# Sliding-window attention and a squared-ReLU MLP on one core: one quarter-megabyte of attention output turned by DMA, in a new order of work

## The chip, the core and the metric

The kernel runs on one core of a Trainium2 chip. A core has TensorE (PE, matrix products and transposes through a 128x128 array), VectorE (DVE), ScalarE (ACT), GpSimd (POOL) and SyncE (SP, which only issues transfers here), and 16 DMA engines. Each engine has its own instruction queue and works through it in order. The metric is the device time of one execution in microseconds (us), lower is better; several runs are made and the median is given.

## The reference

Four batches, eight heads, 768 tokens, head size 64. Each token attends to the 128 latest tokens and to the first four (the sinks). The heads' outputs are put side by side, 512 numbers a token, and go through two matrix products with a squared ReLU between them.

```python
scores = scale * np.matmul(q, k.transpose(0, 1, 3, 2))
keep = is_sink | in_window            # first 4 tokens, or 0 <= i - j < 128
a = softmax(np.where(keep, scores, -1e9))
x = np.matmul(a, v)                   # [4, 8, 768, 64] -> [3072, 512]
h = x @ w_in                          # 512 -> 2048
g = np.maximum(h, 0.0) ** 2
out = g @ w_out                       # 2048 -> 512, float32
```

## The kernel before

**Tiles.** A batch has six tiles of 128 tokens, taken in three pairs, s = 0, 1, 2; tokens 512 to 767 are s = 2. Everything is computed in bf16 and summed in f32.

**Attention of a batch.** Q and K come as [tokens, heads x 64] and must be turned, because a product needs the head dimension on the partitions. For batches 0 and 1 TensorE turns them (`pt`, L642; input `qs` for the first four tiles of batch 0, loaded by SP and cast by DVE, else `qn`, loaded and cast by POOL's queue), and DVE or ACT copies the result to `qkT`. For batches 2 and 3 (`NATURAL`) SP issues a DMA transpose (L596). Then TensorE makes the scores (`ps`, L749; for the first pair of batch 0 with a bias, L742), ACT their exponential (`expm`, L769), DVE or POOL the mask (L778, L781 on DVE; two instructions of L360 on POOL), and TensorE the products with V (`po`, L817), which carry the sum of weights as a 65th column. The sinks have scores of their own (`pk`, L708), exponentials (`es`), and V rows (`vs`, L690). DVE divides by the sum and writes the attention output to `xn_sb` (L833, L834).

**The bridge.** The first product of the MLP needs the attention output with its 512 features on the partitions. For batches 0 and 1 TensorE turns each pair of tiles with eight 128x128 transposes (`px`, L866), and two copies by DVE or ACT bring them to `xT`. For batches 2 and 3 SP issues two DMA transposes for a pair (L848).

**The MLP.** Layer 1 (`pm`, L895) runs in blocks of 128x1024 numbers in PSUM: with two pairs of tokens at once (512 wide, 8 matmuls of 512 columns) or with one (256 wide, 16 matmuls of 256 columns). A block goes through a ReLU (`r`, L906 on ACT, L908 on DVE) and a square (`gT`, L915 on ACT, L917 on DVE). Layer 2 is plain for the first two pairs of batch 0 (`py`, L936) and otherwise a Strassen-like scheme with seven products instead of eight (`py`, L1047; for the very last pair one of them in a bank of its own, `ya`), whose sums and differences (`sg`, `wt`, L1005, L977) and combinations (`u`, `osb`, L1072, L1088, L1095) DVE makes. SP stores each pair of tiles as 512 KB (L959, L1120); the last pair of the last batch is stored in parts (L1113, L1114, L1125, L1129).

**What sets the order.** Every step is an operation in a list, with a key, the engines that may do it and a cost on each, the steps that it comes after and the buffers that it takes. A planner (`Plan.run`) walks through them at build time and always takes the operation that can start first by its own clock, ties by key; where several engines may do a step it takes the one that ends it first. The result is a fixed order for every queue. The planner's clock adds `LATENCY` when a result goes from one engine to another, and gives each DMA a time on its queue, `DMA_LATENCY` and a `margin` of its own:

```python
start = max([t + slack if t > 0 else 0.0, engine.get(e, 0.0)] +
            [a.end + LATENCY + slack for a in o.after if a.engine != e or a.dma] +
            [a.issued for a in o.follow])
...
cand = (round(pick[1] + o.lag, 2), o.key)
...
queue[e] = max([queue.get(e, 0.0), end + DMA_START[e]] + moved) + o.dma
end = queue[e] + DMA_LATENCY + o.margin
```

`PLACES` shifts and stretches the keys of a group of steps and gives it a `lag`; `NUDGES` does so for single operations, by their number in the list. While the planner's clock is below `WARM_UNTIL`, it fills gaps on TensorE with transposes whose results nobody reads (L327).

**The loads.** POOL's queue carries, in this order: V of batch 0 and the four slices of `w_in` (512 KB each) mixed, K and Q of batch 0's tiles 4 and 5 (`load_cast`, 128 KB a tile), the rest of batch 0's V, four parts of `w_out` (512 KB each), K and Q of batch 1's tiles 0 to 3, its V for them, K and Q of its tiles 4 and 5, its last V, then batches 2 and 3. Issues wait once eight of them are under way. `load_cast` gives each of its loads 0.9 us on the queue, and a margin of 1.2 for batch 0, 0.3 for batch 1.

Of the kernel before, what the change touches and what calls it, by code (L numbers as in the profile page):

```python
# [16 lines left out]
LATENCY = 0.135  # L17
# [5 lines left out]
    ('att', 0, 0): (3.3, 1.08, 0.18), ('att', 0, 1): (3.285, 0.47, 0.38), ('att', 0, 2): (-0.2, 1.41, -0.24),  # L23
    ('att', 1, 0): (-1.415, 2.2, -0.42), ('att', 1, 1): (-0.385, 1.02, -0.22), ('att', 1, 2): (6.08, 1.06, 0.36),
    ('att', 2, 0): (-0.225, 0.25, -0.64), ('att', 2, 1): (-1.615, 1.17, -0.58), ('att', 2, 2): (0, 1.02, -0.06),
    ('att', 3, 0): (-0.075, 1.08, 0.1), ('att', 3, 1): (-0.04, 1.04, 0.04), ('att', 3, 2): (1.235, 0.72, 0.98),
    ('ev', 0, 2): (-0.16, 1.15, 0.78), ('ev', 1, 0): (0.585, 0.56, -0.48), ('ev', 1, 1): (0.47, 1.11, 0.24),
    ('ev', 1, 2): (-0.095, 1.18, 0.08), ('ev', 2, 0): (-0.22, 0.93, 0.28), ('ev', 2, 1): (0.015, 1.02, -0.46),
    ('ev', 2, 2): (1.345, 0.4, 1.32), ('ev', 3, 1): (-0.155, 1, 0.08), ('ev', 3, 2): (-0.055, 1.28, -0.44),
    ('l1', 0, 0): (-0.035, 1.27, 0), ('l1', 0, 1): (0.18, 0.85, 0.08), ('l1', 0, 2): (-0.6, 1.31, -0.4),  # L30
    ('l1', 1, 0): (4.96, 0.3, 0.74), ('l1', 1, 2): (0.265, 1.41, -0.28), ('l1', 2, 0): (-0, 0.59, 0.5),
    ('l1', 2, 2): (0.1, 1.22, -0.12), ('l1', 3, 0): (0.075, 0.91, 0.48), ('l2', 0, 0): (0.055, 0.81, 0.38),
    ('l2', 0, 1): (0.435, 1.16, 0), ('l2', 0, 2): (0.16, 1.12, -0.1), ('l2', 1, 0): (1.05, 0.56, -0.96),
    ('l2', 1, 1): (-0.425, 1.06, -0.1), ('l2', 1, 2): (-0.18, 1.03, 0.2), ('l2', 2, 0): (-0.115, 0.96, 0.58),
    ('l2', 2, 1): (2.185, 1.21, 1.32), ('l2', 2, 2): (2.75, 1, 0.74), ('l2', 3, 0): (-0.765, 0.25, 2.4),
    ('l2', 3, 1): (0.08, 0.81, 0.18), ('l2', 3, 2): (0.23, 1.94, 2.82), ('prep', 0, 0): (2.165, 1.2, -0.5),
    ('prep', 0, 1): (0.115, 1.01, -0.24), ('prep', 1, 0): (0.05, 0.87, 0.08), ('prep', 1, 1): (0.84, 1.23, 0.54),
    ('prep', 2, 0): (-0.005, 0.96, 0.24), ('prep', 3, 0): (-0.045, 1.08, 1.16),
    ('sink', 0, 0): (0.015, 1.11, -0.04), ('sink', 0, 1): (0, 1.12, -0.06), ('sink', 1, 0): (-0.225, 1.01, -0.06),
    ('sink', 3, 0): (-0.565, 0.62, 0.5), ('sum', 0, 2): (-0.14, 0.68, -0.34), ('sum', 1, 0): (-1.615, 0.44, -1.74),  # L40
    ('sum', 1, 1): (0.645, 0.91, -1.4), ('sum', 1, 2): (0.34, 1.45, 0.14), ('sum', 2, 0): (-0.655, 1.85, 0.06),
    ('sum', 2, 1): (-0.24, 1, 0.18), ('sum', 2, 2): (0.405, 1.27, 0.3), ('sum', 3, 0): (0.25, 2.36, 0.94),
    ('sum', 3, 2): (0.185, 1.17, 1.74), ('turn', 0, 0): (-0.56, 2.1, -0.62), ('turn', 0, 1): (0.11, 0.94, -0.14),
    ('turn', 0, 2): (-0.205, 1.01, 0.02), ('turn', 1, 0): (-0.2, 0.94, -0.02),
    ('turn', 1, 1): (-0.345, 1.33, -0.42), ('turn', 1, 2): (1.765, 2.5, -2.14), ('turn', 2, 0): (0, 1.05, 0),
    ('turn', 2, 1): (-0.26, 1.09, -0.3), ('turn', 3, 0): (-0.06, 1.05, -0.44), ('turn', 3, 1): (0.075, 0.56, 0.64),
    ('turn', 3, 2): (0, 1, 0.14), ('val', 0, 0): (0.345, 0.45, -0.28), ('val', 0, 1): (0.69, 0.58, -0.46),
    ('val', 0, 2): (-0.09, 0.78, -0.08), ('val', 1, 0): (-2.595, 0.7, 0.22), ('val', 1, 1): (0.035, 1.14, 0.06),
    ('val', 1, 2): (-0.65, 0.98, 0.64), ('val', 2, 0): (-1.11, 0.59, -1.94), ('val', 2, 1): (0.755, 0.42, -0.3),
    ('val', 2, 2): (-0.425, 1.6, -0.06), ('val', 3, 0): (0.1, 1.17, 0.6), ('val', 3, 1): (0.805, 0.25, 0.74),  # L50
    ('val', 3, 2): (0.105, 0.92, 2.28), ('wt', 0): (-0.205, 0.82, -0.32),
}
NUDGES = {
    4: (-0.022, 0.56), 16: (0, 0.14), 17: (-0.211, -0.38), 18: (0.48, -1.62), 19: (0, 0.4), 20: (0.364, -0.58),
    21: (0.004, 0.16), 22: (0.02, 0), 23: (0.016, 0.18), 24: (-0.06, -0.78), 25: (0.35, 1.84), 26: (-0.106, 0.66),
    27: (0.014, -0.64), 29: (-0.004, 0.86), 30: (0, 0.42), 31: (0.013, 0), 33: (-0.009, 0), 34: (-0.094, 0.5),
    36: (-0.027, 0.16), 37: (0.188, 0.08), 38: (-0.052, 0), 39: (-0.269, -0.82), 40: (-0.004, 0),
    41: (-0.419, 0.34), 42: (0.398, -2.86), 43: (0.134, -0.1), 44: (0.027, 0.14), 45: (0.009, 0), 46: (0.123, 0.66),
    47: (0.073, 0.9), 49: (0, 0.1), 51: (-0.102, -0), 52: (-0.278, -0.06), 53: (-0.001, 0.18), 56: (0.05, 0.1),
    57: (0.049, -0.16), 58: (0.016, -0.78), 60: (-0.008, -0.14), 61: (-0.013, 0), 62: (0, 0.22), 63: (-0.292, -0.2),  # L60
    64: (-0.079, 0.34), 65: (0.028, 0.64), 66: (-0.114, -0.38), 67: (0.099, -0.02), 68: (0.076, -0.28),
    69: (-0.851, 0.68), 71: (0.036, 0.22), 72: (-0.036, -0.24), 73: (0.024, 0.18), 74: (0.02, 0), 75: (-0.063, 0),
    76: (0, -0.04), 78: (0.042, 0.28), 80: (0.009, 0.26), 81: (0.023, 1.36), 82: (-0.02, 0.04), 83: (-0.008, -0.54),
    84: (-0.128, -0.42), 85: (-0.161, -0.36), 86: (0.003, 0), 87: (-0.004, 0.08), 88: (-0.069, 0),
    89: (-0.003, -0.16), 90: (-0.088, 0.02), 91: (0.016, -0.28), 92: (0.109, 0), 93: (0.015, 0.38),
    94: (0.043, -0.24), 95: (0.159, 0.04), 96: (-0.083, 0.04), 97: (-0.05, -0.3), 98: (-0.346, 0.8),
    99: (-0.435, 0.54), 100: (-0.21, -0.52), 101: (0.407, 1.44), 102: (0.013, 0.78), 103: (0.147, -0.08),
    104: (-0.112, -0.16), 105: (-0.121, -0.1), 107: (0.009, 0), 108: (0.214, 0.04), 109: (0.006, 0.08),
    111: (0.033, 0.86), 112: (0.046, 0.56), 113: (0.043, 0.6), 114: (-0.154, 0.42), 115: (-0.084, -0.16),
    116: (-0.145, -0.28), 117: (-0.026, -1.22), 118: (0.126, -0.62), 119: (-0.123, -0.24), 120: (0.115, 0.56),  # L70
    121: (0, -0.14), 122: (-0.121, 0.08), 123: (0, -0.2), 124: (0.034, -0.16), 125: (-0.168, 0.24),
    126: (0.017, -0.44), 127: (0.071, -0.82), 128: (-0.128, 0.1), 129: (-0.006, -0.08), 130: (0, -0.56),
    131: (0.402, 0.04), 132: (-0.056, 0), 133: (0.291, -0.28), 134: (-0.028, 0), 135: (0.064, -1.52),
    136: (-0.069, 0), 137: (-0.061, 0.54), 139: (-0.041, 0.32), 140: (-0.043, 0), 142: (-0.077, -0.12),
    143: (-0.069, 0.14), 144: (0.271, 0.26), 145: (0.008, 0.02), 146: (0.046, -0.52), 147: (0.008, -0.22),
    148: (0.006, 0.26), 149: (-0.028, 0.28), 150: (0.065, 0.06), 151: (0.051, 0.04), 152: (0.164, -0.12),
    153: (-0.401, 0.06), 154: (0.019, 0), 155: (-0.388, -0.64), 156: (-0.112, 1.16), 157: (0.287, 0.94),
    158: (-0.278, 1.3), 159: (-0.002, -0.18), 160: (0.118, 0.3), 162: (0.145, 0.5), 164: (0.158, 0.46),
    165: (0.095, 0), 166: (0.015, 0.02), 167: (0.055, 0), 168: (0.161, -0.48), 169: (-0.217, 0.24),
    171: (0.132, 0.52), 172: (0.011, -0.1), 173: (-0.036, 0.78), 174: (-0.047, -0.16), 175: (0.115, 0),  # L80
    176: (-0.342, 0.18), 177: (0, -0.02), 178: (-0.092, 0.58), 179: (0.041, 0.04), 180: (0.136, 0),
    186: (0.353, 0.28), 187: (-0.073, -0.02), 188: (-0.044, 0.48), 189: (-0.009, 0.06), 190: (0.057, -0.6),
    191: (-0.512, 1.18), 192: (0.405, 0.62), 193: (-0.012, -0.02), 194: (-0.003, 0.04), 195: (0.216, 0.94),
    196: (-0.08, -0.04), 197: (-0.038, 0.14), 198: (0.002, -0.54), 199: (0.12, 0.14), 200: (-0.304, 0),
    201: (-0.106, -0.12), 202: (0.038, 0.08), 203: (-0.001, -0.3), 205: (0.013, -0.44), 206: (-0.01, 0.46),
    207: (-0.003, 0.02), 208: (0.277, 0.98), 209: (0.006, -1.42), 210: (0.099, 0.36), 211: (0.041, 0),
    212: (0.006, 0), 214: (0.108, 0.54), 215: (0.057, 0.38), 216: (0.2, 0.22), 217: (-0.118, -0.12),
    218: (-0.002, 0.26), 219: (0.129, -0.22), 220: (0.008, -0.44), 221: (0.213, 1.02), 222: (0.464, -0.34),
    223: (-0.206, 0.1), 224: (0.064, 0), 225: (0.277, 0.32), 226: (-0.123, 0.62), 227: (0.015, 1.76),
# [170 lines left out]
def kernel(  # L260
# [876 lines left out]
    NATURAL, TURNED, BIASED = (2, 3), (), 1  # L1137
# [97 lines left out]
```

The softmax here doesn't subtract the row's maximum and nothing guards it: scores larger than these inputs give would overflow.

## Time and profile before

| | |
|---|---|
| median of 7 runs | 215.46 us (215.07 to 216.59) |
| the profiled execution's own time | 216.06 us |
| its span, first to last instruction | 214.3 us |
| granted TensorE clock | 1.0 of full speed |
| TensorE busy | 207.7 us, 2189 matmuls |
| VectorE, ScalarE, GpSimd busy | 146.8, 118.9, 78.7 us |
| HBM read, written | 27.30 MB, 6.29 MB |
| POOL's DMA queue | 69248 packets, 12.59 MB |

All times of single steps below come from this one profiled execution, counted from the start of its span. A row of the chain of waits has a start, a duration, the engine, the tile and line, and how many instructions were merged. A row of the waits has who waited and for what, then the total, the number and the longest. A row of the DMA issues has the target and source, the issuing queue, the count, the size of one, and the median time from issue to landing. The busy time of TensorE overlaps from one matmul to the next, so the length of a stretch is read from start to start.

### The profile page before, as it was taken

The page shows a single profiled execution, that of the slowest core. Times are in us where ns is not written, and L with a number is a line of the kernel's source. Part 1 is how long each engine was busy: PE and PEld are TensorE (multiplying, and loading weights), DVE is VectorE, ACT ScalarE, POOL GpSimd, SP SyncE. Part 2 cuts the span into 40 slices and gives each one's busy share as a digit, 9 for nine tenths or more (in the row PEclk, how much of TensorE's full clock was granted, in tenths as well). Part 3 has the DMA queues.
Part 4 walks back from the last instruction along what each step waited for, and adds up shares of the span by engine and source line. Part 5 has one row for each costly group of instructions (what it writes and reads, how often), then busy time and mean ns, then how long its engine had stood idle before and what let it go on. Part 6 is the DMA issues. An engine that isn't in the chain of part 4 may idle for free.

```text
span 214.3 us, 5184 instructions
## 1 busy us (share of the span) xinstructions
PE 207.7 (97%) x2189; PEld 161.1 (75%) x2189; DVE 146.8 (69%) x282; ACT 118.9 (55%) x149; POOL 78.7 (37%) x112
## 2 busy tenths in 40 slices
PE   7999999999999999999999999999999999999993
PEld 7568996689487645678897955876997955798892
DVE  6488558577958784677778757648886653476853
ACT  3697457455664669977654379768206036671110
POOL 7989375499969830884800000000000100000000
PEclk9999999999999999999999999999999999999999
DMA  5999999999999999999999543000423160000222
GB/s 161 280 163 204 176 198 213 162 133 204 156 148 149 208 214 124 141 120 162 93 195 161 150 96 101 3 0 0 52 81 93 74 150 0 0 3 2 98 101 98
DMA packets 93351, 26.06 MB, mean 122 GB/s; under 512 B 86800, under 2 KB 91280, under 8 KB 93328
## 3 DMA queue, kind: packets, MB, share of 16 engines
q0 software_dynamic: 69248, 12.59, 83.0%
q1 hardware_dynamic: 23896, 13.07, 29.0%
q8 instruction: 17, 0.28, 0.6%
q10 hardware_dynamic: 184, 0.07, 0.1%
q14 instruction: 6, 0.05, 0.1%
HBM read 27.30 MB, written 6.29 MB: 157 GB/s over the span
## 4 chain that ended last, share of the span: by engine, by line
PE 88%; DMA 6%; ACT 2%; DVE 1%; POOL 1%; SPq 0%; issue 0%
PE pm L895 38%; PE py L1047 28%; PE py L936 7%; PE po L817 6%; PE ps L749 5%; DMA w_in_sb<-in_moe_w_in_dram 4%; PE pt L642 2%; DMA qr<-in_k_dram 2%; ACT expm L769 1%; PE ya L1047 1%; PE px L866 1%; DVE xT L336 1%; PE pk L708 1%; POOL expm L360 1%; SPq L491 0%
## 5 line engine op out<-in xcount | busy, mean ns | idle before, releaser
L895 PE MATMUL pm<-xT,w_in_sb 128*128 128x256 bf16 (+1 forms) x576 | 87.4, 309 | 0.8 <-DMA w_in_sb<-in_moe_w_in_dram 0.6
L895 PEld LDWEIGHTS <-w_in_sb 128*128 128x128 bf16 x576 | 62.4, 114 | 20.8 <-issue 1.3
L906 ACT ACTIVATE r<-pm 128x1024 bf16<-128x1024 f32 x42 | 43.1, 1025 | 32.7 <-PE pm L895 30.5
L769 ACT ACTIVATE expm<-ps 128x1024 bf16<-128x1024 f32 (+1 forms) x48 | 43.4, 953 | 15.5 <-PE ps L749 15.5
L917 DVE TENSOR_TENSOR gT<-r 128x1024 bf16<-128x1024 bf16 x35 | 24.2, 691 | 22.8 <-ACT r L906 22.6
L360 POOL TENSOR_SCALAR_AFFINE_SELECT expm<-expm 128x512 bf16<-128x512 bf16 x12 | 7.3, 635 | 74.2 <-ACT expm L769 68.9
L1047 PEld LDWEIGHTS <-gT 128*128 128x128 bf16 x336 | 31.1, 98 | 4.5 <-issue 1.2
L1047 PEld LDWEIGHTS <-sg 128*128 128x128 bf16 x240 | 22.9, 98 | 3.0 <-issue 0.5
L781 DVE TENSOR_TENSOR expm<-expm,tri 128x1024 bf16<-128x1024 bf16 x26 | 18.3, 706 | 7.7 <-ACT expm L769 7.5
L1047 PE MATMUL py<-wt,gT 128*128 128x256 bf16 x160 | 20.8, 273 | 0.0
L1047 PE MATMUL py<-wt,sg 128*128 128x256 bf16 x160 | 20.8, 273 | 0.0
L1047 PE MATMUL py<-w_out_sb,gT 128*128 128x256 bf16 x144 | 18.7, 273 | 0.0
L834 DVE TENSOR_TENSOR xn_sb<-po,rc 128x512 bf16<-128x512 f32 (+1 forms) x28 | 17.2, 615 | 1.0
L817 PEld LDWEIGHTS <-expm 128*128 128x128 bf16 x352 | 16.3, 97 | 1.9 <-issue 0.4
L817 PE MATMUL po<-v,expm 128*128 128x65 bf16 x352 | 17.3, 193 | 0.2 <-DVE xT L336 0.2
L334 ACT ACTIVATE osb<-py 128x256 f32<-128x256 f32 (+1 forms) x15 | 6.6, 441 | 16.8 <-PE py L1047 11.7
L936 PE MATMUL py<-w_out_sb,gT 128*128 128x512 bf16 x64 | 15.7, 380 | 0.0
L749 PE MATMUL ps<-qkT 64*128 64x128 bf16 (+1 forms) x256 | 14.6, 238 | 0.0
L749 PEld LDWEIGHTS <-qkT 64*128 64x128 bf16 x256 | 8.0, 94 | 8.1 <-issue 7.5
L915 ACT ACTIVATE gT<-r 128x1024 bf16<-128x1024 bf16 x13 | 13.7, 1056 | 0.3
L817 PE MATMUL po<-vs,es 128*128 128x65 bf16 x128 | 13.0, 193 | 0.0
L817 PEld LDWEIGHTS <-es 128*128 128x128 bf16 x128 | 11.7, 97 | 0.0
(78 smaller groups left out, 241.5 us busy)
## 6 DMA issues: line engine op xcount, KB each, us to landing
out_dram<-osb SPq DMA_DIRECT2D x11, 512.0 KB, 3.9
v<-in_v_dram POOLq DMA_DIRECT2D x24, 128.0 KB, 6.6
qn<-in_k_dram POOLq DMA_DIRECT2D x20, 128.0 KB, 7.7
qn<-in_q_dram POOLq DMA_DIRECT2D x20, 128.0 KB, 7.8
w_in_sb<-in_moe_w_in_dram POOLq DMA_DIRECT2D x4, 512.0 KB, 9.3
w_out_sb<-in_moe_w_out_dram POOLq DMA_DIRECT2D x4, 512.0 KB, 11.0
qr<-in_k_dram SPq DMA_DIRECT2D x4, 256.0 KB, 5.1
qr<-in_q_dram SPq DMA_DIRECT2D x4, 256.0 KB, 4.9
```

What stands on the lines that cost most here:

```text
L360: nc.gpsimd.affine_select(out=e_tile, in_=e_tile, compare_op=ALU.is_ge, fill=fill, base=i - 1, pattern=[[0, n], [1 if i else -1, 128]], ch ...
L749: nc.tensor.matmul(ps[:, h2, o:o + w], lhsT=qkT_sb[r, m, 1, c, :], rhs=qkT_sb[r, m, 0, qb:qb + w // 128, :], start=(i == 0 and not biased) ...
L769: nc.scalar.activation(out=x[:, :, o:512], in_=bank_t["s", b, s, m][:, :, o:512], func=AF.Exp, scale=scale)
L781: nc.vector.tensor_mul(y, y, tri.rearrange("p (o a) c -> p o (a c)", o=1).to_broadcast([128, 4, 256]))
L817: touch(("po", b, s, m0), e, nc.tensor.matmul(pv[:, i, h2, :], lhsT=lhsT, rhs=rhs, start=(n_ == 0), stop=(n_ == len(mms) - 1)), j)
L834: touch(("po", b, s, m0), e, nc.vector.tensor_tensor(out=xn_sb[:, 2 * s:2 * s + 2, 128 * (m0 + j0):128 * (m0 + j0 + nj)].rearrange("p i (j ...
L895: nc.tensor.matmul(pm[:, i, :], lhsT=w_in_sb[:, fb // 4, kb, fb % 4:512:4], rhs=xT[:, c0 // 256:(c0 + cw) // 256, kb, :], start=(kb == 0), ...
L906: nc.scalar.activation(out=o, in_=h, func=AF.Relu)
L915: nc.scalar.activation(out=g, in_=r, func=AF.Square)
L917: nc.vector.tensor_mul(g, r, r)
L936: touch((b, u), e, nc.tensor.matmul(pm[:, i, :], lhsT=gT_sb[t // 4][:, fb, 128 * (t % 4):128 * (t % 4) + 128], rhs=w_out_sb[:, fb, :], sta ...
L1047: ins = nc.tensor.matmul(y_, lhsT=x[:, i, :], rhs=r_, start=(first or tail and n == 2) and i == 0, stop=i == HB - 1, skip_group_check=not ...
```

## The change

Three things change in the text of the kernel.

The attention output of batch 1, s = 2 (tokens 512 to 767) is no longer turned on TensorE but by two DMA transposes on SP's queue, in the way of batches 2 and 3. The eight `px` transposes and the two copies of that pair go. In the planner's clock these two transfers get a margin of 10.0 us.

`LATENCY` goes from 0.135 to 0.222.

`PLACES` and `NUDGES` are new throughout, so that the order on every queue differs.

```diff
-LATENCY = 0.135
+LATENCY = 0.222
 PE_SLACK = 0.0
 DMA_START = {"sp": 1.45, "act": 1.2, "pool": 1.6}
 DMA_LATENCY = 0.9
 WARM_UNTIL = 34.0
 PLACES = {
-    ('att', 0, 0): (3.3, 1.08, 0.18), ('att', 0, 1): (3.285, 0.47, 0.38), ...
+    ('att', 0, 0): (-0.04, 0.71, -0.12), ('att', 0, 1): (0, 1.77, 0), ...
...
 NUDGES = {
-    4: (-0.022, 0.56), 16: (0, 0.14), 17: (-0.211, -0.38), ...
+    16: (0.046, -0.46), 17: (0.032, 1.14), 18: (-0.001, -0), ...
...
                         o_ = op(at(fs + 0.36), {"sp": 1.25}, turn_x, dma=0.3, after=norms + older_layer1 +
                                 ([o_] if t % 2 else []))
-                        o_.margin = 2.284
+                        o_.margin = 10.0 if b == 1 else 2.284
...
-    NATURAL, TURNED, BIASED = (2, 3), (), 1
+    NATURAL, TURNED, BIASED = (2, 3), (2,), 1
```

How the new order differs, by queue:

- **TensorE.** The same matmuls but for the eight `px`; 70 filler transposes instead of 61. Up to the third slice of `w_in` the same steps in nearly the same order. After it three layer-1 blocks instead of four stand ahead of the 16 transposes of Q and K of batch 0's tiles 4 and 5. The 16 transposes of batch 1's tiles 4 and 5 move from just ahead of layer 1 of batch 1 to the middle of the plain layer 2 of batch 0, and batch 1's s = 2 is attended first instead of with the others. Scores are reached from layer-1 or layer-2 matmuls 21 times instead of 20. At the end the last two pairs of tiles are mixed: four products of the last but one stand between the last pair's, and its final one just ahead of the last `ya`.
- **POOL.** The loads keep their order. One Q piece is cast here instead of on DVE; the third and fourth slices of `w_in` are issued ahead of the first two mask instructions instead of behind them. 24 mask instructions instead of 12 (12 tiles instead of six).
- **SP.** The first new transpose stands after the first four of batch 2's Q and K and ahead of the second store of batch 0; the second after that store and four more of batch 2's.
- **ACT and DVE.** ReLUs 38 and 10 instead of 42 and 6; squares 16 and 32 instead of 13 and 35; masks on DVE 32 instead of 38; copies to `xT` 5 and 5 instead of 3 and 9.

## The prediction

> **What bounds the kernel now.** I read the engine table first, then the slices, then the chain of waits in order of time, the waits of TensorE, and last the landing times of single loads.
>
> ```profile
> PE 207.7 (97%) x2189; PEld 161.1 (75%) x2189; DVE 146.8 (69%) x282; ACT 118.9 (55%) x149; POOL 78.7 (37%) x112
> ...
> PE   7999999999999999999999999999999999999993
> ...
> DMA  5999999999999999999999543000423160000222
> ```
>
> TensorE is busy from the second slice to the last; the DMA engines are full from slice 2 to 21, about 5 to 115 us. Any TensorE time that goes or comes counts one for one; a load that is late for its transpose stops TensorE itself. The chain shows which work stands where:
>
> ```profile
> 13.98 8.86 DMA w_in_sb<-in_moe_w_in_dram
> 22.89 7.18 PE pm L895 x64
> 30.07 0.89 PE pt L642 x16
> ...
> 42.96 0.45 PE px L866 x8
> ...
> 52.59 1.34 PE pt L642 x24
> ...
> 72.26 0.91 PE pt L642 x16
> ...
> 209.87 0.91 PE ya L1047 x16
> ```
>
> Until 22.89 the third slice of w_in sets the pace. The 16 transposes at 30.07 turn Q and K of batch 0's tiles 4 and 5, those at 72.26 the same of batch 1; the eight px at 42.96 are one bridge (attention output turned on TensorE). All TensorE waits of 0.2 us or more on others:
>
> ```profile
> PE pt L327 <- POOL ident L384: 1.5, 1, 1.5
> PE pm L895 <- DMA w_in_sb<-in_moe_w_in_dram: 0.6, 2, 0.4
> PE pt L642 <- DVE qs L336: 0.3, 1, 0.3
> PE pm L895 <- DVE xT L336: 0.2, 1, 0.2
> PE px L866 <- DVE xn_sb L834: 0.2, 1, 0.2
> PE pt L327 <- ACT expm L769: 0.2, 1, 0.2
> PE po L817 <- DVE xT L336: 0.2, 1, 0.2
> ```
>
> After 22.89 only two are left, some 0.35 us together. Now the loads. POOL's timeline has the last Q load of batch 0 issued at 19.96 and that of batch 1 at 49.67; the DMA view for 20.84 to 20.86 and for 50.55 to 50.60 gives their time to landing:
>
> ```profile
> qn<-in_q_dram POOLq DMA_DIRECT2D x1, 128.0 KB, 9.7
> ```
>
> ```profile
> qn<-in_q_dram POOLq DMA_DIRECT2D x1, 128.0 KB, 6.8
> ```
>
> So they land at 29.66 and 56.47. The kernel before asks for them at 29.91 and 72.1: the first has 0.25 us to spare, the second 15.6.
>
> **What the Trainium skill says.** "DMA: Bandwidth & Descriptors", Anatomy of one DMA, has about 2 us fixed and then bytes by bandwidth, and semaphores waited for before issue, so that the engines just consume their queues. Here 128 KB loads take 5.3 to 12.5 us: most of that is standing in line. The same page, Issuing engines are not separate DMA queues, says that all issuers share 16 engines. The trace agrees: POOL's queue moved 0.15 MB in the microsecond from 49, and 0.05 from 51, when an output store (issued by SP at 47.99) moved. "TensorE: Matmul & The Clock Gate", Part 4, has a PE transpose near 275 ns with a copy out of PSUM after it; here one takes 219 ns and they start 55 ns apart, and the copies are 422 ns (DVE) or 595 ns (ACT).
>
> **The change part by part.**
>
> *Turned by DMA.* Eight px go: 0.45 us (one row of the chain). Two xT copies go too, on engines with room: nothing. SP gets two transposes of 1.24 us. In its queue the first stands after batch 2's first four Q/K turns and ahead of an output store; the second stands after that store and four more turns. The store waits for batch 0's second pair of tiles, which my count below puts near 71; four turns of 1.29 bring 76, its own issue 77.3, landing (median 3.2, longest 4.9) at most 82.2. The layer-1 blocks that read it start near 95. Cover 13 us: priced at nothing; if it were gone, each microsecond would count. What the second transpose delays are batch 2's later turns. Its tiles 2 and 3 go ahead of it, end on SP near 76 and land (longest 8.8) by 85, their scores being due near 89.
>
> *The new order, up to 22.89.* POOL casts one Q piece itself (nearest row: its 128x512 copy, 0.61) and issues w_in slices 2 and 3 ahead of its first two masks instead of after. Issue is earlier by 1.4 us by my count of POOL's rows. I give it nothing: slice 2 was issued at 13.98, 6.3 us before slice 1 landed (10.54 + 9.7 = 20.24), and landed 2.6 us after it; the queue never ran dry, and its order is the same. The attention steps ahead of the first layer-1 block end about 0.4 us later, by their rows; TensorE idled 0.41 at the next w_in wait, which takes that.
>
> *The new order, 22.89 to 57.* This decides. The third w_in slice lands at 22.89 in both. Then the new order has three layer-1 blocks ahead of the 16 transposes of batch 0, not four. A block of 16 is 1.755 (64 in 7.02 to the next start): TensorE is there at 28.16. The last Q lands at 29.66. Thirteen of the 16 transposes stand at or behind that load: 29.66 + 13 x 0.055 = 30.4, against 28.16 + 0.89 = 29.05 unstopped. **Loss 1.35.**
>
> The 16 of batch 1 move far forward. Between 22.89 and them the new order has 9 blocks (15.8), 8 L936 parts of 0.87 (7.0), 48 transposes (2.7), scores in two x12 and two x8 groups (0.55 and 0.44, 2.0), two pk (0.6), 48 po (1.45), a bridge (0.45), and six changes from wide matmuls to scores or pk, each 0.10 (an L936 part ahead of scores is 0.97, not 0.87). Sum 30.5: arrival 53.4, or 54.7 after the first loss. The last Q lands at 56.47; thirteen transposes more, 57.2, against 54.3 unstopped. **Second loss 1.6, together 2.9.** The loads' order on POOL is the same and the store that cuts in (near 50.5 now, 47.99 before) still moves ahead of the last Q; if it moved behind, the landing would be some 0.9 earlier. The planner has these loads 0.9 us apart and no store among them; the trace has 0.95 and the store. Ends: 1.7 (landing 0.9 earlier and 0.3 from POOL's earlier issue) to 3.2.
>
> Batch 1's tile-3 Q lands at 42.66 + 5.3 = 47.96, where TensorE asks near 47.9: no more than 0.1.
>
> *The rest.* One more change from wide to scores: +0.1. The 0.35 of waits need not come back: -0.3. Six masks move from DVE (0.71 each) to POOL (two of 0.64 each): 7.6 us more on POOL, ahead of batch 3's loads. By its rows the last Q load of batch 3 issues near 115.5, lands by 122, and is turned and landed by 130, against sinks due near 136: nothing, and later than that microsecond for microsecond. Relus and squares shift between ACT and DVE, both under 70%: nothing. New short waits behind these chains aren't shown by this trace: 0 to 1.0; below nothing is excluded, since the waits left are 0.35. I take 0, TensorE being 2.9 later and other engines not.
>
> *The tail.* Before, the last two 64 KB stores are issued about 0.3 after the last matmul (210.77) and land 2.0 later. Now a 512 KB store of another tile pair is among the last. Its final product ends 0.89 ahead of the last matmul; the old trace has 1.08 from such an end (198.50) to the store (199.58): issue 0.2 after the end, then 0.33 on SP, its data 0.7 to 2.3 after issue. The last half's store is behind it. +0.2 to +0.7, I take 0.4.
>
> **Sum**: -0.45 + 0.1 - 0.3 + 2.9 + 0.4 = +2.7 on a span of 214.3, so 217.0. The profiled execution took 216.06, which is 1.8 over its span and 0.6 over the median: 218.8, and in medians 215.46 + 2.7 = **218.2**.
>
> **Rivals.**
>
> *Paced by issue, faster.* If POOL's issue sets the landings, w_in comes up to 1.4 earlier, its two waits (0.6) go, and the loads come before TensorE asks: -0.45 + 0.1 - 0.3 + 0.4 - 0.6 = -0.85, **214.6**. It decides once batch 1's last Q lands by 53.5, three microseconds earlier. For it: from 43 to 50 issues are 0.88 apart, near the landings' 0.95. Against: the DMA row stands at 9 throughout, and the queue is the same.
>
> *The waits small, no change.* The landing is early enough to leave about 0.3 of wait: -0.45 + 0.1 - 0.3 + 0.4 + 0.3 = +0.05, **215.5**.
>
> *A late turn on top.* If SP's order held back the turned output by over 13 us, or batch 2's tiles by over 4, each further microsecond adds: with one, **219.2**. The covers speak against it.
>
> That the change doesn't do what it says is excluded by the instruction lists: eight px fewer, two SP transposes more.
>
> **How the numbers follow.** About 0.3% (0.65 us) is what a measurement tells from no change. The two load waits 0.75, late turns on top 0.05, so slower 0.80; no change 0.10; faster 0.10. The likeliest gives 218.2, its own range 216.7 to 219.2 (losses 1.7 to 3.2, tail 0.2 to 0.7, new waits to 0.5). The range for 8 in 10 reaches down into the no-change case, 215.6, and up to 219.5, with late turns.
>
> **What would show it.** Right: TensorE waits for DMA qn of about 1.3 to 1.5 near 28 to 30 and near 55 to 56.5, the last Q of batch 1 landing at 56 to 56.5; px x40; the span's end about 3.9 after the last matmul. Wrong: no such wait and that load landing by 53.5; or a wait on xT or qkT after 85 of over 0.5, which would be the turns.

## The result and the profile after

The changed kernel takes 218.2 us (median; 217.27 to 219.27), the kernel before 215.82 beside it; the ratio is 1.011, 95% interval 1.009 to 1.0131, so 2.4 us slower. The forecast was 218.2. The profiled execution took 218.23 with a span of 216.5, against 216.06 and 214.3: 2.2 in the spans. The total came out, but the traces of the two kernels don't show the loss where the prediction looked for it.

The page of the changed kernel, engine table and slices (all its line numbers are 6 below those of before):

```profile
PE 207.2 (96%) x2190; PEld 160.6 (74%) x2190; DVE 147.2 (68%) x277; ACT 117.5 (54%) x145; POOL 87.8 (41%) x125
...
PE   7869999999999999899999999999999999999991
...
DMA  4999999999999999999999961300160112000213
```

TensorE is busy 0.5 us less than before although the span is 2.2 longer: the px went, and idle time came. By the slices, 5.4 us each, the second and third (5.4 to 16.2 us) fell from 9 to 8 and 6, the last from 3 to 1. The chain of waits, in order of time, has these steps:

```profile
7.11 6.92 DMA v<-in_v_dram
18.57 1.87 PE pm L889 x16
...
24.15 5.24 PE pm L889 x48
29.44 0.91 PE pt L636 x16
...
54.71 1.00 PE pt L636 x16
...
87.78 1.03 ACT r L900
...
210.92 0.69 DVE osb L1089
```

In this execution the front (all up to the third w_in slice's first block) is no longer paced by w_in but by a V load; three layer-1 blocks (x48) stand ahead of the 16 transposes of batch 0, and the 16 of batch 1 are at 54.7, both as worked out. All TensorE waits of 0.2 us or more:

```profile
PE po L811 <- DMA v<-in_v_dram: 1.5, 1, 1.5
PE pt L321 <- POOL ident L378: 1.5, 1, 1.5
PE pm L889 <- ACT r L900: 0.6, 1, 0.6
PE pt L636 <- POOL qs L331: 0.5, 1, 0.5
PE pt L636 <- DVE qs L330: 0.2, 1, 0.2
```

No wait on qn at all. Batch 0's last Q lands near 29.4 (before 29.7). TensorE begins the 16 transposes at 29.28 and comes to the fourth, the first that may need this load, only near 29.45. Batch 1's last Q lands 5.9 after its issue at 48.53, at 54.4 (before 56.5), and TensorE asks at 54.64:

```profile
qn<-in_q_dram POOLq DMA_DIRECT2D x1, 128.0 KB, 5.9
```

The difference of the two spans by stretches needs two starts more of the changed kernel, from its timeline:

```profile
23.98 5.40 PE L889 MATMUL pm<-xT,w_in_sb 128*128 128x256 bf16 x48
...
210.72 1.06 PE L1041 MATMUL ya<-w_out_sb,gT 128*128 128x128 bf16 x16
```

The third w_in slice's block starts at 23.98 instead of 22.89: +1.1. From there to the last matmul's end (211.78, before 210.77) 187.8 against 187.9: -0.1. From that end to the span's end 4.7 against 3.5: +1.2. Theory A at this point: the front and the tail are the loss. Theory B: the load queue is, and a front that is late by chance hid that in this execution.

### The profile page after: what moved, and what is told of

The parts are those of the page before. It is cut to its first block, busy times and chain, and to the rows that moved or that the text cites. A ratio compares the mean times of both kernels' runs of the same rounds, so it can differ in the third digit from the quotient of the medians.

```text
span 216.5 us, 5205 instructions
## 1 busy us (share of the span) xinstructions
PE 207.2 (96%) x2190; PEld 160.6 (74%) x2190; DVE 147.2 (68%) x277; ACT 117.5 (54%) x145; POOL 87.8 (41%) x125
## 3 DMA queue, kind: packets, MB, share of 16 engines
q1 hardware_dynamic: 24984, 13.33, 30.7%
## 4 chain that ended last, share of the span: by engine, by line
PE 90%; DMA 3%; DVE 2%; POOL 1%; issue 1%; ACT 0%; DVEq 0%; POOLq 0%; ACTq 0%
PE pm L889 39%; PE py L1041 28%; PE po L811 7%; PE py L930 7%; PE ps L743 5%; DMA v<-in_v_dram 3%; PE pt L636 2%; PE px L860 1%; POOL vs L684 1%; PE pk L702 1%; POOL v L515 1%; ACT r L900 0%; DVE vs L368 0%; PE ya L1041 0%; DVE xn_sb L828 0%
## 5 line engine op out<-in xcount | busy, mean ns | idle before, releaser
L900 ACT ACTIVATE r<-pm 128x1024 bf16<-128x1024 f32 x38 | 38.8, 1022 | 30.4 <-PE pm L889 27.7
L911 DVE TENSOR_TENSOR gT<-r 128x1024 bf16<-128x1024 bf16 x32 | 22.3, 696 | 16.8 <-ACT r L900 16.6
L354 POOL TENSOR_SCALAR_AFFINE_SELECT expm<-expm 128x512 bf16<-128x512 bf16 x24 | 16.3, 712 | 31.6 <-ACT expm L763 29.5
L909 ACT ACTIVATE gT<-r 128x1024 bf16<-128x1024 bf16 x16 | 16.8, 1056 | 0.3
L775 DVE TENSOR_TENSOR expm<-expm,tri 128x1024 bf16<-128x1024 bf16 x20 | 14.0, 702 | 3.9 <-ACT expm L763 3.3
L902 DVE TENSOR_SCALAR r<-pm 128x1024 bf16<-128x1024 f32 x10 | 12.2, 1222 | 3.3 <-PE pm L889 3.3
L827 DVE RECIPROCAL rc<-po 128x8 f32<-128x8 f32 (+1 forms) x28 | 5.5, 196 | 12.8 <-PE po L811 12.7
```

What stands on the lines that cost most here:

```text
L354: nc.gpsimd.affine_select(out=e_tile, in_=e_tile, compare_op=ALU.is_ge, fill=fill, base=i - 1, pattern=[[0, n], [1 if i else -1, 128]], ch ...
L775: nc.vector.tensor_mul(y, y, tri.rearrange("p (o a) c -> p o (a c)", o=1).to_broadcast([128, 4, 256]))
L900: nc.scalar.activation(out=o, in_=h, func=AF.Relu)
L909: nc.scalar.activation(out=g, in_=r, func=AF.Square)
L911: nc.vector.tensor_mul(g, r, r)
```

## The experiments

In the experiments the planner's picks are written out as a list (one entry per step: index, engine, banks) and replayed, so that an edit moves only what it names; AFTER and BEFORE are the lists of the two kernels, with the changed one's numbering. The list moves the line numbers by about a hundred: layer-1 products are L990 or L991 there, transposes of Q and K L737 or L738. Differences in us are differences of ratios times 215.5; where an interval is given with them it is the two ratios' own, joined by squares.

**The front of before.**

```diff
-ORDER = AFTER
+ORDER = BEFORE[:117] + [LOAD_34] + AFTER[118:]
```

> The changed kernel with the order and the engines of the kernel before up to the third w_in slice's first layer-1 block, all after it as changed. Theory A (read from the two traces: the front lost 1.1 us in the attention chain, no load gates TensorE later): 217.1 us, that block starting near 22.9, no wait for a Q or K load over 0.3. Theory B (the prediction's step: the last Q load of batch 0 gates the transposes as soon as TensorE comes early): the block starts near 22.9, but a wait for DMA qn of 1.0 to 1.4 stands before the transposes near 28 to 29.5, and the time stays near 218.2.

Ratio 1.0109 (1.008 to 1.0138): no gain at all, within 0.8. In its trace the third block starts at 22.96, a microsecond earlier than in the changed kernel, and the last matmul ends 0.7 earlier. Theory A's time fell, B's came out. The wait that B foretold did not show here: batch 0's last Q landed at 28.62 in this execution, and the 16 transposes just took 1.31 us instead of 1.07.

**The tail of before.**

```diff
-ORDER = AFTER
+ORDER = AFTER[:680] + BEFORE[682:]
```

> The changed kernel with the last 80 steps in the order and on the engines of the kernel before: the last pairs' products one pair after the other, not mixed. Theory A (the traces: the tail lost 1.2 us): 217.0 us, the span ending 3.5 after the last matmul. Theory B (the prediction's 0.4, the rest being execution to execution): 217.8, the span ending 3.5 to 4.3 after it.

Ratio 1.0093 (1.0062 to 1.0124), 0.4 less than the changed kernel, with an interval of 0.8 either way: the time alone doesn't separate the theories, and the 3.75 from the last matmul to the end of its own trace suits both. All the traces together say more. These are the last steps outside TensorE of the changed kernel, from its timeline (start, us, engine):

```profile
210.92 0.69 DVE L1089 TENSOR_TENSOR osb<-py,u 128x512 f32<-128x512 f32 x1 [0.86 <-PE py L1041]
211.53 0.41 DVE L330 COPY osb<-py 128x256 f32<-128x256 f32 x1
211.81 0.28 ACT L328 ACTIVATE half<-ya 128x128 f32<-128x128 f32 x1 [6.62 <-PE ya L1041]
211.85 0.28 DVE L330 COPY osb<-ya 128x128 f32<-128x128 f32 x1
211.97 0.33 SPq L1114 DMA_DIRECT2D out_dram<-osb  x1
212.12 0.35 ACTq L1108 DMA_DIRECT2D out_dram<-half  x1
212.39 0.38 SPq L1107 DMA_DIRECT2D out_dram<-osb  x1
```

and of the kernel with the tail of before:

```profile
210.70 0.33 SPq L1224 DMA_DIRECT2D out_dram<-osb  x1
211.20 0.28 DVE L431 COPY osb<-ya 128x128 f32<-128x128 f32 x1
211.31 0.33 SPq L1220 DMA_DIRECT2D out_dram<-osb  x1
211.48 0.28 ACT L429 ACTIVATE half<-ya 128x128 f32<-128x128 f32 x1 [3.13 <-PE ya L1142]
211.74 0.38 SPq L1208 DMA_DIRECT2D out_dram<-osb  x1
211.79 0.35 ACTq L1209 DMA_DIRECT2D out_dram<-half  x1
```

In the changed kernel the 512 KB store of the other pair goes out at 211.97, the 64 KB of the last half behind it on SP and beside it in the DMA engines. In the other the large stores are issued by 211.31. Of the five traces with the changed tail, four end 4.7 after their last matmul and one 4.4; the nine with before's tail 3.5 to 3.8. So by the traces the mixed tail costs about 1.0. The times gave 0.4 here and 0.5 with the front put back too (the next experiment against the first), within 0.8 and 0.9: 1.0 is in reach of both, but they don't show it.

**Both at once.**

```diff
-ORDER = AFTER
+ORDER = BEFORE[:117] + [LOAD_34] + AFTER[118:680] + BEFORE[682:]
```

> The changed kernel with both the front and the tail of the kernel before; of the change only the middle is left. Theory A (front and tail are all of the loss): 215.9 us, no different from the kernel before, or 0.1 better. Theory B (load waits appear once the front is early): 217.0 or more, with a wait for DMA qn near 28 to 29.5 and one near 53 to 55. Theory C (the prediction without its load waits): 215.2, the middle alone being 0.65 better.

Ratio 1.0084 (1.0052 to 1.0117): most of the loss is still there. TensorE's waits in its trace:

```profile
PE pt L737 <- DMA qn<-in_q_dram: 2.0, 4, 0.7
PE pt L422 <- POOL ident L479: 1.5, 1, 1.5
PE po L912 <- DMA v<-in_v_dram: 0.9, 1, 0.9
PE pm L990 <- ACT r L1001: 0.6, 1, 0.6
```

The wait on qn is there, 2.0 us. (This execution took 218.61, the longest of its six, whose median is 217.29; so the waits are those of an unlucky one.) Its timeline says where:

```profile
28.77 0.23 PE L737 MATMUL pt<-ident,qn 128*128 128x128 bf16 x1 [0.66 <-DMA qn<-in_q_dram]
29.35 0.90 PE L737 MATMUL pt<-ident,qn 128*128 128x128 bf16 x13 [0.36 <-DMA qn<-in_q_dram]
...
47.97 0.23 PE L737 MATMUL pt<-ident,qn 128*128 128x128 bf16 x1 [0.23 <-DMA qn<-in_q_dram]
48.94 0.68 PE L737 MATMUL pt<-ident,qn 128*128 128x128 bf16 x9 [0.74 <-DMA qn<-in_q_dram]
```

The first pair is the prediction's first wait, with 13 transposes behind the last load as it said. The second pair is at batch 1's tile-2 and tile-3 Q, not at its last Q. Theory A fell; theory B stands, with another second place.

**The load queue lightened**, on this kernel, on the changed one, and on the kernel before as a control.

```diff
             "pool", ("w_in", i),
-            lambda e: [nc.gpsimd.dma_start(
+            lambda e: [] if i == 3 else [nc.gpsimd.dma_start(
...
-                    nc.tensor.matmul(pm[:, i, :], lhsT=w_in_sb[:, fb // 4, kb, fb % 4:512:4],
+                    nc.tensor.matmul(pm[:, i, :], lhsT=w_in_sb[:, min(fb // 4, 2), kb, fb % 4:512:4],
```

> Front and tail of the kernel before, middle of the changed one, and the load of the fourth w_in slice left out (its products take the third slice's weights, so the output is another): 512 KB less in the load queue from about 23 us on, every later load some 2.5 us earlier. Theory A (in that kernel TensorE waits for loads at the early transposes, 2.0 us in its trace): those waits go, 215.3 to 215.8. Theory B (the waits are chance, the loss is elsewhere): 217.3 as with the load.

> The kernel before with the load of the fourth w_in slice left out in the same way (its products take the third slice's weights). The control: TensorE there waits for no load behind that slice, the last Q load of batch 0 having 0.25 us to spare. Theory A: no change, 215.3, at most 0.3 less. Theory B (a lighter queue helps any order alike): 1.5 to 2 less, as in the kernel beside it.

> The changed kernel itself, whole order, with the load of the fourth w_in slice left out (its products take the third slice's weights). Theory A (in the changed kernel too the load queue paces TensorE at the early transposes in a usual execution, a late front only standing in for it): 1.0 to 1.8 less, 216.3 to 217.1. Theory B (what was lost in the front's chain of attention steps is the loss, loads matter only once the front is mended): 0.3 less at most, 217.8 or more.

| kernel | with the load | without it | difference, us |
|---|---|---|---|
| before | 1 | 1.0003 (0.9982 to 1.0024) | +0.1, within 0.5 |
| front and tail of before | 1.0084 (1.0052 to 1.0117) | 0.9999 (0.9983 to 1.0015) | -1.8, within 0.8 |
| changed kernel | 1.011 (1.009 to 1.0131) | 1.0062 (1.004 to 1.0084) | -1.0, within 0.7 |

Theory A in all three. Batch 0's last Q lands at 26.2 to 26.5 there instead of 28.6 to 29.9, and no wait on qn is left. These are TensorE's waits of the second kernel without the load, to be held against the list with it:

```profile
PE pt L422 <- POOL ident L479: 1.5, 1, 1.5
PE pt L738 <- DVE qs L431: 1.0, 2, 0.7
PE pm L991 <- ACT r L1002: 0.6, 1, 0.6
PE pt L422 <- ACT expm L865: 0.3, 1, 0.3
PE po L913 <- DMA v<-in_v_dram: 0.2, 1, 0.2
```

The order of before gains nothing from a lighter queue, the new one gains one to two microseconds: the loads pace the new order. In the changed kernel the effect is smaller than with the front mended, as if a late front stood in for part of the load wait; but the difference of the two differences, 0.8, is within its uncertainty of 1.0, so that much stays open.

**The bank.** A layer-1 block is summed in one of a few PSUM buffers (banks), and can go to one only when the relu that reads it is done. In the changed kernel's list relu 339 stood ahead of relu 318, so the layer-1 block at 88.85 was given the bank that 339 (ScalarE, 87.78 to 88.80) reads, though the other had been read by 87.39.

```diff
-    (339, 'act', ('r',), ...), (318, 'dve', ('r',), ...),
+    (318, 'dve', ('r',), ...), (339, 'act', ('r',), ...),
```

> The changed kernel with two neighbouring steps of its list exchanged, relu 339 on ScalarE and relu 318 on VectorE, so that the layer-1 block after them gets the bank that is read first; no engine's own order changes. Theory A (the 0.62 us wait for a relu at 88.85 is a cost of the new order's bank choice): the wait goes and the time falls by 0.6 to about 217.5. Theory B (the wait only stands where another would): it comes back within the next 10 us and the time stays near 218.1.

> Front and tail of the kernel before, the exchanged bank of after_bank, and the load of the fourth w_in slice left out. Everything found so far is taken away together, so only the turn and the middle's order are left. Theory A (the losses are the loads, the bank and the tail, and they add up): 0.6 less than without the exchange, 215.0, some 0.6 below the kernel before with the same load left out. Theory B (something is lost that is not found yet): 215.4 or more.

The first: ratio 1.0084 (1.005 to 1.0117) against 1.011; the second 0.9979 (0.9962 to 0.9997) against 0.9999. That is 0.6 and 0.4 less, each time with this wait gone from the trace and none in its place; each interval alone still reaches zero (0.8 and 0.5 either way). Theory A in both, by the traces and by the size. The second kernel is 0.5 below the kernel before with the same load left out, within 0.6: that is the turn by DMA and the middle's order by themselves.

**The turn alone, both ways.** First the kernel before with only the turn; then the changed order with the bridge back on TensorE.

```diff
-    NATURAL, TURNED, BIASED = (2, 3), (), 1
+    NATURAL, TURNED, BIASED = (2, 3), (2,), 1
...
-ORDER = BEFORE
+ORDER = BEFORE with bridge 270, 272 and copies 271, 273 replaced by turn_x 270, 271 on SP
```

> The kernel before, its order kept, with only batch 1's output of tokens 512 to 767 turned by two DMA transposes on SP in place of eight px. In the order of before the output is normalized by 91.26 and TensorE reads it turned from 93.12. Theory A (the turn needs the new order): two issues of 1.2 us each and a landing put it near 95 to 96.5, TensorE waits 2 to 3.5 us for xT, 217.0 to 218.5. Theory B (the turn is hidden, as it is in the changed kernel): 215.0, 0.45 less than before.

Ratio 1.0367 (1.0331 to 1.0403): 7.9 us slower, theory A, and more than twice its size of 1.5 to 3.0. The timeline of TensorE, and the windows (us, then busy time and instructions of PE, PEld, DVE, ACT, POOL; granted clock; DMA share; GB/s):

```profile
98.47 2.94 PE L989 MATMUL pm<-xT,w_in_sb 128*128 128x256 bf16 x13 [5.71 <-DMA xT<-xn_sb]
```

```profile
88.00:92.00 4.00, 4.00 (x45) 2.44 (x44) 2.14 (x4) 3.83 (x4) 4.00 (x6) 1.00 2.66 148
...
98.50:101.00 2.50, 2.50 (x13) 1.76 (x14) 0.00 (x0) 0.00 (x0) 0.00 (x0) 0.50 1.73 182
101.00:104.00 3.00, 3.00 (x23) 1.84 (x22) 0.00 (x0) 1.91 (x2) 0.00 (x0) 0.53 0.69 137
104.00:108.00 4.00, 4.00 (x39) 3.76 (x38) 1.93 (x3) 2.32 (x4) 1.20 (x3) 1.00 0.00 0
```

The turns took 5.5 to 5.8 us from issue to landing, where the expectation left 1 to 3 behind the two issues. And after 5.71 idle TensorE was granted only 0.50 of its clock up to 101 and 0.53 up to 104: 2.5 x 0.50 + 3.0 x 0.47, some 2.7 us more. So the turn needs the attention of those tiles to come far earlier, as it does in the new order, at the price of early loads.

```diff
-    NATURAL, TURNED, BIASED = (2, 3), (2,), 1
+    NATURAL, TURNED, BIASED = (2, 3), (), 1
...
-ORDER = AFTER
+ORDER = AFTER with turn_x 270, 271 replaced by bridge 270, 272 and copies 271, 273
```

> The changed kernel's order with batch 1's output of tokens 512 to 767 turned on TensorE again: eight px and two copies put where the first of the two DMA transposes stood. Theory A (the turn is hidden and worth its eight px): 0.45 more, 218.5. Theory B (the px fall into time that TensorE loses anyway, or the two transposes on SP cost something): within 0.2 of the changed kernel, or less.

Ratio 1.014 (1.0109 to 1.017), 0.65 more than the changed kernel, within 0.8: theory A's sign and size, though not apart from zero. In its trace the load waits stand without any of before's order (transposes of batch 0, then tile 3 of batch 1):

```profile
28.80 0.90 PE L737 MATMUL pt<-ident,qn 128*128 128x128 bf16 x13 [0.54 <-DMA qn<-in_q_dram]
...
48.04 0.68 PE L737 MATMUL pt<-ident,qn 128*128 128x128 bf16 x9 [0.69 <-DMA qn<-in_q_dram]
```

The front up to here is that of the changed kernel, step for step. So in an execution of the same steps the predicted first wait was there. The traced one of the changed kernel missed it with a front that was late for at least one reason of chance: V's second tile landed at 14.03 (7.11 and 6.92 in its chain). In the 14 traces of this study that load is issued between 6.83 and 7.18 and lands between 12.13 and 14.03, latest of all in the changed kernel's; the three others with its front and all loads had 12.32, 12.36 and 12.83, but 13.75 came up with before's front too.

**Mending the gates by order.** A gate is a load that TensorE has to wait for. On the kernel with both ends of before and the bank exchanged, first w_in's fourth slice behind batch 0's last Q:

```diff
-POOL: w_in 24, 25, 26, K and Q of tiles 4 and 5 27, 28, 29, 30, v 31
+POOL: w_in 24, 25, K and Q of tiles 4 and 5 27, 28, 29, 30, w_in 26, v 31
...
-PE: layer-1 block 177 (slice 3), transposes 128, 131, layer-1 block 165 (slice 1)
+PE: layer-1 block 165 (slice 1), transposes 128, 131, layer-1 block 177 (slice 3)
```

> Front and tail of the kernel before, the exchanged bank, and, with every load kept, the fourth w_in slice loaded behind the last Q of batch 0 and two layer-1 blocks exchanged so that it is used after the transposes. Q of batch 0 lands some 2.5 us earlier, Q of batch 1 when it did. Theory A (the first load gate costs 0.7 to 1.0, the second stays): 217.3 - 0.6 - 0.8 = 215.9. Theory B (what the first gate gives is lost at the second, near 47 to 49): 216.6. Theory C (both gates go): 215.2.

Ratio 1.0064 (1.0041 to 1.0087), theory B: 1.4 above before, where the bank alone would leave 1.3. The last Q of batch 0 landed at 26.8 and that wait is gone, but the next one stands:

```profile
48.18 0.68 PE L737 MATMUL pt<-ident,qn 128*128 128x128 bf16 x9 [0.69 <-DMA qn<-in_q_dram]
```

So Q of batch 1 was given work to hide behind (282 and 283 are layer-2 parts, the rest transposes; one copy of theirs goes from ScalarE to VectorE with it):

```diff
-PE: 282, 197, 193, 201, 283, scores 212, 204, 205
+PE: 282, 283, 197, 193, 201, 204, 205, scores 212
```

> As late_w_in3, and batch 1's Q transposes of tiles 0 to 3 put behind the last layer-2 part of that stretch (0.87 us of work that needs no load), the fourth pair's transposes pulled ahead of the scores, so that TensorE asks for tile 3's Q near 48.7 to 49 instead of 47.5. Theory A (the second gate is what took back the first one's gain): the wait of 0.7 on that load goes, the time falls by 0.5 to 0.7 against late_w_in3, ratio 1.003 to 1.004, 216.3. Theory B (the time is lost once more, on the copies ahead of the scores or at the last Q near 54 to 55.5): ratio 1.0055 or more, with a new wait in one of these places.

Ratio 1.0072 (1.0045 to 1.0099): theory B once more. The wait near 48 is gone, and this came in its place, in order of time:

```profile
55.12 0.23 PE L737 MATMUL pt<-ident,qn 128*128 128x128 bf16 x1 [0.99 <-DMA qn<-in_k_dram]
56.04 0.23 PE L737 MATMUL pt<-ident,qn 128*128 128x128 bf16 x1 [0.69 <-DMA qn<-in_q_dram]
57.02 0.68 PE L737 MATMUL pt<-ident,qn 128*128 128x128 bf16 x9 [0.75 <-DMA qn<-in_q_dram]
```

That is the prediction's second wait at its place, 2.4 us, the last Q landing at 57.0. (This execution took 218.78, against a median of 217.2.) Two things came together here. The output store, issued at 48.50 instead of 50.10, moved ahead of these loads; for the microsecond from 51 the queues show (packets, MB, share)

```profile
q1 hardware_dynamic: 79, 0.32, 86.1%
q0 software_dynamic: 212, 0.03, 41.7%
```

where the changed kernel has 0.15 MB on q0 and nothing on q1. And POOL issued the last of batch 1's first four Q loads at 43.41 instead of 41.31, because the sink values ahead of it took twice their time, 3.62 instead of 1.80:

```profile
39.84 3.62 POOL L785 TENSOR_TENSOR vs<-vs_in,head_rows 32x130 bf16<-32x130 f32 x4
```

No version that keeps all its loads beats the kernel before.

## Why the prediction was right, and where not

*TensorE's arrival.* Right. It put the batch-0 transposes 5.27 after the third slice's block; they came 5.30 after (23.98 to 29.28). From that block to batch 1's it worked out 30.5 without a wait; they came 30.7 after it. That the time itself agrees, 54.64 against 54.7, is luck: the delay ahead of them was the front's 1.1 and not the first wait.

*The first load wait, 1.35.* Right as a mechanism and in its place, but too large: 1.0 in the kernel with both ends of before, 0.54 in the one with the bridge, none in the traced execution of the changed kernel, whose front was late by 1.1. Batch 0's last Q lands anywhere from 28.6 to 29.9 in the eight traces that keep all loads in their order; the one landing taken from the trace of before, 29.66, was among the late ones.

*The second, 1.6.* The step that failed. It carried the landing of 56.47 over from before and let it come earlier by 1.2 at most. It came 2.0 earlier, and without a wait: the load was issued at 48.53 instead of 49.67, 1.1 earlier where 0.3 was allowed, and took 5.9 instead of 6.8. In the kernel before POOL issued no load between 38.98 and 42.66, and from 44 to 47 its queue moved only 0.08 to 0.13 MB per us; in the changed one the gap was 38.48 to 41.31 and the queue moved 0.14 to 0.15, some 0.1 MB more, or about 0.7 us. So by these two traces the issue counted at this place, as the faster rival had it, though not for w_in, whose third slice was issued 1.4 earlier and landed at 23.15 instead of 22.84. The store still moved mostly ahead of that landing, as the prediction had it: 0.09, 0.29 and 0.12 MB in the microseconds from 52, 53 and 54 (before 0.21, 0.25 and 0.06 from 50, 51 and 52). How the rest of the 2.0 divides stays open. The 0.1 for tile 3's Q at 47.9 failed the other way: that wait was 0.4 to 1.0 in four of the eight traces with the new middle and all loads. Together the loads cost 1.0 in the changed kernel and 1.8 with its front and tail put back (within 0.7 and 0.8), not 2.9.

*The front, priced at nothing.* The nothing was right for the time as far as the runs tell: putting before's front back gained 0.0, within 0.8. In the traced execution the steps did end later, by 1.1 where 0.4 was worked out, but one trace is a poor witness here. The third slice's block starts at 22.63 to 24.35 in the five traces with the changed front and at 22.24 to 24.45 in the nine with before's; V's second tile came late in some of both, and once w_in's third slice (landing at 24.30). What the order itself adds is TensorE's wait for the Q cast that moved to POOL, 0.4 to 0.5 in four of the five traces with this front and in none of the others. The prediction let the w_in wait take the delay; the traces show other takers, and what the cast costs in the end is not shown.

*New short waits, 0 to 1.0, taken as 0.* Undersized: the bank costs 0.4 to 0.6, its wait 0.62.

*The tail, 0.4.* Undersized: about 1.0 by the traces. The prediction saw the 512 KB store among the last. It did not count that the last tile's copy stands behind the other pair's on VectorE, so that its store on SP is issued 0.61 after the last matmul's end instead of 0.28; and it gave the small stores too little for company in the DMA engines: the 64 KB on ACT's queue took 2.9 to land instead of 2.1.

*The rest*, -0.45 + 0.1 - 0.3 = -0.65: measured -0.5, within 0.6.

The sum of these terms is -0.5 + 0.5 + 1.0 + 1.0 = 2.0 against 2.4 measured and 2.7 forecast: a load term about 1.9 too large, and a tail and a bank together about 1.1 too small. By the ratios alone, one experiment after the other, it is 0.6 for front and tail, 1.8 for the loads, 0.4 for the bank and -0.5 for the rest, each within 0.5 to 0.8, with 0.1 for the control. The two ways split loads and ends differently, and these runs can't tell which is nearer.

So the mechanism, loads that pace the new order, is right; that the total came out to the tenth is luck. The errors of the terms went opposite ways and left 0.3, and the median of before, 215.46 when the forecast was made, was 215.82 in the comparison.

*The rivals.* The faster one was to decide once batch 1's last Q landed by 53.5; it landed at 54.4, ahead of TensorE, and the kernel was not faster for it. The late turn didn't occur: no wait on xT anywhere in the changed kernel, where the second turn is issued near 76 and takes 9.7 to land. That is 85.6, where at most 82.2 was worked out; the cover took it.

## What to carry to other kernels

When a reordering brings work forward to just behind its loads, take the landing times as a band over executions and not from one trace, and list every load that the new order comes close to: removing one gate here only uncovered the next. Leaving one load out, on both kernels, tells in two runs whether an order is paced by its loads, even where the trace at hand shows no such wait. Read a tail from the last matmul to the end separately, over several traces, and ask which large store and which copies the new order puts in front of the last small ones.

## What the runs showed of the hardware

- In an idle stretch of 5.71 us TensorE's granted clock fell to half some 4 us in, and stayed there for 5.3 us of work after it (96.98 to 103.81). The Trainium skill, "TensorE: Matmul & The Clock Gate", Part 1, has an idle window bring the clock to half rate until a busy window has passed; this trace agrees. Shorter waits went both ways: after one of 1.62 us on V, in the kernel with both ends of before, the bank exchanged and the load left out, the clock was 0.50 from 15.25 to 18.66; after one of 1.51 in the same place of the changed kernel it stayed at 1.0.
- A store on SP's queue nearly stopped POOL's loads in the microsecond in which it moved most: 0.03 MB (before: 0.05) against 0.15. The skill, "DMA: Bandwidth & Descriptors", Queues, rings and completion order, has each DMA engine take turns between queues by packet; here the store's packets averaged 4 KB (0.32 MB in 79) and the loads' 0.13 KB (0.15 MB in 1151). That fits in kind: a turn of the store's moves some 30 times a load's. But 212 load packets went beside the 79, so the turns were not one for one throughout.
- Four small GpSimd products took 3.62 us instead of 1.80 where VectorE's 128x2048 subtractions ran beside them (from 40.64; in the changed kernel these began at 42.02, after them): the two that overlapped took 1.32 and 1.27, the two others 0.40 and 0.42. "GPSIMD Engine Reference", Specifications, says that the two engines share their SBUF interfaces, with contention when VectorE has two SBUF inputs; the trace agrees, but no run tried it alone.
- A DMA transpose of 128x512 took 5.5 to 5.8 us from issue to landing in the kernel before with the turn, and 9.7 in the changed kernel (issued at 75.89).
